# One core, gated linear attention into a gated FFN: all engines' orders, PSUM banks and holds laid out anew

## The chip, the cores and the metric

One core of a Trainium2 chip runs the program. It has five engines with instruction queues of their own: PE (TensorE, matmuls), DVE (VectorE), ACT (ScalarE), POOL (GpSimd) and SP (SyncE, here for DMAs only). The time is the device time of one execution in microseconds; the median of three executions is compared.

## What is computed

Two stages; the output of the first is the input of the second.

```python
B, H, S, D = 4, 8, 768, 48
f = 1.0 / (1.0 + np.exp(-f_logit))
for t in range(S):
    state = f[:, :, t, :, None] * state + np.einsum('bhd,bhe->bhde', k[:, :, t], v[:, :, t])
    y[:, :, t] = np.einsum('bhd,bhde->bhe', q[:, :, t], state)
...
x = attn_out.transpose(0, 2, 1, 3).reshape(3072, 384)
gate = np.maximum(x @ w_gate, 0.0)
val = x @ w_val
return gate * val @ w_out
```

d_model is 384, d_ff is 1536, all inputs are float32.

## The kernel before

**Tiling.** The 768 positions are cut into six chunks of 128. Chunk c of batch b is one piece of work, named by two digits (12 is chunk 1, batch 2). Chunks 0 and 1 are handled in *units* of two pieces: unit 0.0 is pieces 00 and 01, unit 0.2 is 02 and 03, then 1.0 and 1.2. Each unit needs one load of 384 KB of each of f, k, q and v (`load`, L407 for these, L412 for later chunks). The weights come in ten *slices* (`load_w`, L434), all issued by POOL: wg0+2 is columns 0 and 1 (of 12 blocks of 128) of w_gate, wv4+4 is blocks 4 to 7 of w_val, wo is w_out.

**Stages of a piece**, with the names that the orders use:

- `ef`, `ln` (ACT, L483 and L486): log of the forget gate, for two pieces at once; `cum` (PE, L504 or L513): its running sum
- `ek`, `eq` (ACT, L527 and L529): exponentials of the sum; `hk`, `hq` (POOL or DVE, L551 or L552): k and q scaled by them, called hats
- `tk`, `tq` (PE, L563) and `ck`, `cq` (DVE or ACT): transposes and their copies, chunks 0 and 1 only; later chunks use a DMA transpose `xh` (SP, L571)
- `s` (PE, L661 or L595): scores; `m` (DVE): masks; `v` (POOL, DVE or ACT, L581 to L583): v cast to bfloat16
- `kv` (PE): the state's update, `st`, `ss`, `sd`: the new state; `y`, `yi` (PE, L683, L719, L756): the output; `x`: its copy, turned, as input of the FFN
- `g` and `u` (PE, L803): the two projections of a hidden block, 00.6 being block 6 of all of chunk 0; `r` (ACT or DVE): the relu, `p` (DVE, L811): the product; `o` (PE, L824): the output projection in three parts; `d` and `S`: its copy and its store

In chunk 0 blocks 0 to 3 are done for two pieces at a time (256 columns, names g00.x and g02.x, *narrow*), all others for four (512 columns, *wide*).

**Order.** Every instruction group is an `Op` with a number. `ORDER` lists for each engine which numbers it runs, in which order. Engines run strictly in that order. From it `Plan.lay_out` (L153) takes the engine of each Op, and `BANKS` says which of the eight PSUM banks each newly opened result of PE takes; an Op that opens a bank waits for whoever still reads the bank's last tenant. `Plan.waits` (L187) works out the semaphore waits. `HELD` adds waits that the data do not need: an Op number and the Op that it is held for. An entry like ~4512 in PE's list is a *filler* (L884 to L890): four matmuls of 512 columns on zeros, whose result is thrown away; before a filler PE waits for the readers of the bank it writes. The list starts with ~60100, 60 fillers of 100 columns.

**Loads.** In the kernel before, SP and ACT send unit loads at the same time: SP f0.0, q0.0, f0.2, v0.2, k0.2, f1.0, f1.2, q1.2, then k1.0, q1.0, k1.2; ACT v0.0, k0.0, q0.2, ahead of its first arithmetic. k1.0 and k1.2 are held for slice wv4+4, f1.0 for wg2+2, v1.2 for wo0+4; five slices (wg0+2, wv0+2, wv2+2, wv4+4, wo0+4) are held for loads in turn.

Of the kernel before, what the change touches and what calls it, by code (L numbers as in the profile page):

```python
# [25 lines left out]
        45, ~60100, 85, 74, ~4512, 92, ~4512, 82, 90, 80, 101, ~3512, 95, 121, 110, ~7512, 100, 118, 104, 126, 128, 152, 156,  # L26
        137, 116, 230, 131, ~4512, 266, 148, 241, 150, 144, 146, ~2512, 136, 140, 277, 158, 154, 168, 170, 184, 164, 166,
# [13 lines left out]
    ],  # L41
    "ACT": [
# [8 lines left out]
    ],  # L51
    "DVE": [
# [901 lines left out]
```

## Time and profile before

| | us |
|---|---|
| median of 3 runs | 193.23 (192.92 to 193.8) |
| span of the profiled execution | 193.3 |
| granted TensorE clock | 1.000 of full speed |

The page gives the span from the first to the last instruction of the profiled execution and no other time for it; the span lies within 0.1 us of the runs' median. In 40 slices of 4.8 us each, busy tenths of PE and DVE, and GB/s moved:

```profile
PE   7889999879999999999999999999999999999994
...
DVE  5288867898968999758896779799788974585431
...
GB/s 148 285 319 265 170 196 212 149 219 245 209 238 188 233 198 254 172 178 231 242 180 233 212 235 225 173 215 91 108 196 120 2 41 0 46 0 81 41 43 123
```

PE is busy nearly all the time after the first nine slices. Matmuls are pipelined and fillers count as busy, so a busy PE is not yet a useful one. The chain of waits, read below, is the list of what released what, followed back from the last instruction. The view of a line's DMA issues gives the time from the issue to the landing.

### The profile page before, as it was taken

Reading aid. Unit: us, or ns where it says so; the run is one execution under the profiler, and the core shown is the slowest. Engines: PE = TensorE matmul, PEld = TensorE weight load, DVE = VectorE, ACT = ScalarE, POOL = GpSimd, SP = SyncE. Lnnn points to the kernel's source line nnn. Section 1 sums busy time; section 2 is a strip of 40 time slices with the busy share of each in tenths; the row PEclk is TensorE's granted clock in tenths of the full one; section 3 lists DMA queues with packets and bytes.
Section 4 is the critical chain, followed back from the end, with each engine's and each line's share of the span. In section 5 each row is a group of like instructions: output and inputs, shape, how many; then the busy total and the mean of one; then the engine's idle time right before and its main releaser. Section 6 shows DMA issues by size and latency. Waiting matters only on the chain.

```text
span 193.3 us, 4847 instructions
## 1 busy us (share of the span) xinstructions
PE 185.0 (96%) x1989; PEld 109.6 (57%) x2007; DVE 146.6 (76%) x271; ACT 86.7 (45%) x188; POOL 49.6 (26%) x78
## 2 busy tenths in 40 slices
PE   7889999879999999999999999999999999999994
PEld 7555675455565555655556565556655655555562
DVE  5288867898968999758896779799788974585431
ACT  2768963530388541588603797223352311113200
POOL 8368600420053300044623244161140000000000
PEclk9999999999999999999999999999999999999999
DMA  5999998699999999789999999896564010102113
GB/s 148 285 319 265 170 196 212 149 219 245 209 238 188 233 198 254 172 178 231 242 180 233 212 235 225 173 215 91 108 196 120 2 41 0 46 0 81 41 43 123
DMA packets 110279, 32.44 MB, mean 168 GB/s; under 512 B 103472, under 2 KB 110000, under 8 KB 110256
## 3 DMA queue, kind: packets, MB, share of 16 engines
q1 hardware_dynamic: 92032, 25.04, 60.2%
q0 software_dynamic: 3744, 3.54, 11.4%
q10 hardware_dynamic: 14480, 3.54, 8.1%
q8 instruction: 16, 0.26, 0.5%
q14 instruction: 7, 0.06, 0.1%
HBM read 25.95 MB, written 4.72 MB: 159 GB/s over the span
## 4 chain that ended last, share of the span: by engine, by line
PE 79%; DMA 11%; POOL 3%; ACT 2%; DVE 2%; issue 1%; SPq 0%; ACTq 0%
PE ps L803 41%; PE ps L824 25%; DMA wv<-in_moe_w_val_dram 5%; DMA q_in<-in_q_dram 4%; PE ps L595 2%; DMA f_in<-in_f_logit_dram 2%; PE ps L756 2%; POOL hats L551 2%; PE ps L513 2%; DVE hats L552 2%; PE ps L563 1%; PE ps L783 1%; PE ps L661 1%; PE ps L767 1%; POOL wg L434 1%
## 5 line engine op out<-in xcount | busy, mean ns | idle before, releaser
L811 DVE TENSOR_TENSOR gT<-relu,ps 128x512 bf16<-128x512 bf16 (+1 forms) x76 | 48.9, 654 | 15.8 <-PE ps L803 9.9
L803 PE MATMUL ps<-xT,wv 128*128 128x512 bf16 (+1 forms) x223 | 56.9, 368 | 0.4
L803 PE MATMUL ps<-xT,wg 128*128 128x512 bf16 (+1 forms) x218 | 55.4, 367 | 0.5
L824 PE MATMUL ps<-wo,gT 128*128 128x384 bf16 (+2 forms) x300 | 52.1, 320 | 0.0
L808 ACT ACTIVATE relu<-ps 128x512 bf16<-128x512 f32 (+1 forms) x42 | 23.9, 571 | 41.6 <-DVE gT L811 24.3
L824 PEld LDWEIGHTS ps<-wo,gT 128*128 128x128 bf16 x300 | 27.2, 98 | 18.7 <-DVE gT L811 0.6
L803 PEld LDWEIGHTS ps<-xT,wg 128*128 128x128 bf16 x228 | 23.6, 108 | 19.3 <-ACT xT L608 0.2
L803 PEld LDWEIGHTS ps<-xT,wv 128*128 128x128 bf16 x228 | 23.4, 108 | 18.7 <-ACT osb L830 0.5
L809 DVE TENSOR_SCALAR relu<-ps 128x512 bf16<-128x512 f32 (+1 forms) x34 | 22.3, 663 | 6.7 <-PE ps L803 5.9
L603 DVE TENSOR_TENSOR ptm<-ps,tri 128x512 bf16<-128x512 f32 x32 | 19.9, 683 | 2.6 <-PE ps L595 2.5
L459 POOL TENSOR_TENSOR st<-ssum,dec 128x384 bf16<-128x384 f32 x10 | 8.6, 856 | 33.4 <-DVE ssum L457 33.3
L551 POOL TENSOR_TENSOR hats<-q_in,expo 128x384 bf16<-128x384 f32 x13 | 13.7, 1060 | 12.8 <-ACT expo L529 8.1
L830 ACT ACTIVATE osb<-ps 128x384 f32<-128x384 f32 (+1 forms) x13 | 6.2, 480 | 21.2 <-PE ps L824 21.2
L529 ACT ACTIVATE expo<-ps 128x384 f32<-128x384 f32 x24 | 11.7, 496 | 7.9 <-PE ps L513 3.3
L551 POOL TENSOR_TENSOR hats<-k_in,expo 128x384 bf16<-128x384 f32 x11 | 11.4, 1038 | 13.2 <-ACT expo L527 10.2
L483 ACT ACTIVATE f_in<-f_in 128x768 f32<-128x768 f32 x12 | 10.0, 840 | 8.5 <-DMA f_in<-in_f_logit_dram 5.2
L552 DVE TENSOR_TENSOR hats<-k_in,expo 128x384 bf16<-128x384 f32 x13 | 10.9, 850 | 2.4 <-ACT expo L527 2.0
L527 ACT ACTIVATE expo<-ps 128x384 f32<-128x384 f32 x24 | 11.8, 499 | 1.5 <-PE ps L504 0.9
L552 DVE TENSOR_TENSOR hats<-q_in,expo 128x384 bf16<-128x384 f32 x11 | 7.0, 642 | 5.7 <-ACT expo L529 4.8
L888 PE MATMUL ps<-zeros 128*128 128x100 bf16 (+1 forms) x81 | 10.7, 309 | 0.3 <-issue 0.2
L668 DVE TENSOR_TENSOR ptm<-ps,tmask 128x512 bf16<-128x512 f32 x16 | 10.0, 683 | 0.6 <-PE ps L661 0.6
L486 ACT ACTIVATE bneg<-f_in 128x768 bf16<-128x768 f32 x12 | 10.1, 838 | 0.1
(79 smaller groups left out, 161.6 us busy)
## 6 DMA issues: line engine op xcount, KB each, us to landing
out_dram<-osb SPq DMA_DIRECT2D x23, 192.0 KB, 2.5
f_in<-in_f_logit_dram SPq DMA_DIRECT2D x10, 384.0 KB, 6.3
q_in<-in_q_dram SPq DMA_DIRECT2D x10, 384.0 KB, 5.9
k_in<-in_k_dram SPq DMA_DIRECT2D x10, 384.0 KB, 5.4
v_in<-in_v_dram SPq DMA_DIRECT2D x9, 384.0 KB, 5.8
v_in<-in_v_dram ACTq DMA_DIRECT2D x3, 384.0 KB, 5.1
k_in<-in_k_dram ACTq DMA_DIRECT2D x2, 384.0 KB, 6.7
q_in<-in_q_dram ACTq DMA_DIRECT2D x2, 384.0 KB, 7.7
```

The source lines that it names most:

```text
L486: add(f"ln{c}{b0}", by("ACT", lambda: sc.activation(bo, fl, AF.Ln, bias=1.0), act_(n)), keys + [f"bneg{bi}"], [f"bn{bi}_{x % 2}" for x in ...
L527: add(f"ek{c}{b}", by("ACT", lambda: sc.activation(ex[:, 1, :], bc.ap[:, 0:HD], AF.Exp, scale=1.0), act_(HD)), [bc], [f"expk{ei}"], key=P + 1)
L529: add(f"eq{c}{b}", by("ACT", lambda: sc.activation(ex[:, 0, :], bc.ap[:, 0:HD], AF.Exp, scale=-1.0), act_(HD)), [bc], [f"expq{ei}"], key=P ...
L551: return {**by("POOL", lambda: gp.tensor_tensor(o, i_, e_, ALU.mult), pool_(HD)), **by("DVE", lambda: ve.tensor_tensor(o, i_, e_, ALU.mult ...
L552: **by("DVE", lambda: ve.tensor_tensor(o, i_, e_, ALU.mult), dve_(HD))}
L603: add(f"m{c}{b}{j}", by("DVE", lambda b=b, j=j, mi=mi: ve.tensor_tensor(ptm[mi][:, j, :, :], s[b, j].ap[:, :].rearrange("p (n t) -> p n t" ...
L803: z = te.matmul(bank.ap[:, 0:n], wt[:, kt, w_cols(j)], xT[xi][:, kt, n0:n1], start=(kt == 0), stop=(kt == NK - 1))
L808: add(f"r{c}{b0}.{j}", {**by("ACT", lambda: sc.activation(rdst, gate.ap[:, 0:n], AF.Relu), act_(n)), **by("DVE", lambda: ve.tensor_scalar_ ...
L809: **by("DVE", lambda: ve.tensor_scalar_max(rdst, gate.ap[:, 0:n], 0.0), dve_(n))}, [gate], [f"relu{ri}"], key=P)
L811: add(f"p{c}{b0}.{j}", by("DVE", lambda: ve.tensor_tensor(gT[gi][:, j, n0:n1], rdst, val.ap[:, 0:n], ALU.mult), dve_(n)), [val, f"relu{ri} ...
L824: z = te.matmul(o.ap[:, 0:e1 - e0], gT[gi][:, j, b * C:(b + 1) * C], wo[:, j, e0:e1], start=(j == 0), stop=(j == NJ - 1))
L888: te.matmul((op.opens[0].ap if op.opens else banks[7])[:, 0:fill % 1000], zeros[:, 0:128], zeros[:, 0:fill % 1000], start=True, stop=True, ...
```

## The change

Only the three tables change; no Op is added or removed and none computes anything else. 11 of the 24 wide fillers go. The number of Ops per engine: DVE 271 to 266, POOL 74 to 82, ACT 180 to 179, SP 88 to 86, PE the same.

```diff
 ORDER = {
     "PE": [
-        45, ~60100, 85, 74, ~4512, 92, ~4512, 82, 90, 80, 101, ~3512, 95, 121, 110, ~7512, 100, 118, 104, 126, 128, 152, 156,
-        137, 116, 230, 131, ~4512, 266, 148, 241, 150, 144, 146, ~2512, 136, 140, 277, 158, 154, 168, 170, 184, 164, 166,
+        45, ~60100, 85, 74, ~3512, 110, 90, ~2512, 80, 121, 82, 92, ~3512, 95, 116, 126, 128, ~2512, 101, ~1512, 118,
+        ~1512, 100, 104, 230, 131, 266, 152, ~1512, 148, 137, 241, 144, 136, 140, 238, 158, 156, 172, 160, 154, 186,
...
     "POOL": [
-        41, 40, 25, 1, 36, 37, 38, 2, 4, 3, 13, 5, 7, 14, 8, 11, 56, 16, 39, 17, 20, 26, 94, 84, 79, 52, 120, 106, 125, 51,
-        57, 114, 62, 63, 69, 68, 142, 70, 71, 281, 280, 262, 298, 416, 382, 385, 408, 424, 441, 560, 558, 525, 566, 532, 565,
+        41, 25, 7, 39, 13, 16, 4, 26, 11, 38, 8, 1, 14, 5, 56, 17, 20, 78, 114, 36, 124, 2, 3, 37, 94, 84, 40, 115,
+        51, 57, 130, 63, 120, 52, 235, 62, 68, 106, 69, 70, 245, 71, 234, 244, 281, 280, 270, 276, 385, 262, 383, 390,
...
     "SP": [
-        46, 48, 50, 55, 53, 58, 64, 66, 59, 60, 65, 374, 61, 222, 517, 510, 373, 370, 212, 217, 803, 375, 384, 425, 417, 227,
+        46, 50, 47, 48, 53, 54, 49, 58, 55, 60, 59, 66, 368, 372, 371, 370, 212, 369, 375, 374, 373, 514, 510, 384,
...
 HELD = {
-    51: 53, 52: 50, 57: 53, 58: 56, 59: 63, 63: 58, 65: 63, 67: 70, 70: 60,
+    372: 378, 516: 343,
 }
```

The same in names, up to where the prediction walks (loads start with L; ~n is n wide fillers):

```text
SP before:   Lf0.0 Lq0.0 Lf0.2 Lv0.2 Lk0.2 Lf1.0 Lf1.2 Lq1.2 Lk1.0 Lq1.0 Lk1.2 Lq2.2 Lv1.0 S02
SP after:    Lf0.0 Lf0.2 Lk0.0 Lq0.0 Lk0.2 Lq0.2 Lv0.0 Lf1.0 Lv0.2 Lq1.0 Lk1.0 Lq1.2 Lf2.0 Lf2.2
             Lv2.0 Lq2.0 S00
ACT before:  Lv0.0 Lk0.0 Lq0.2 ef00 ln00 ek01 eq01 ek00 eq00 dc00 cq01 ef02 ck00 ln02 v03 ek03 eq03
ACT after:   ef00 ln00 ef02 ek01 ln02 ek00 eq01 eq00 ek02 eq03 ek03 cq00 Lf1.2 eq02 dc02 ck03 ef10
             dc00 ln10 ef12 ln12 x01 ek10 dc12 eq10 dc10 ek12 r00.2 r00.1 eq12 r00.0 x03 ek11 eq11
             eq13 r02.3 Lk1.2 r00.4 ek13 r00.6 r00.8 r00.11 ck11 cq13 ef20 ln20 Lv1.0 Lv1.2 ek20
             eq21 eq20 dc20 dc21 v10 ek21 d01 v13 d00 ef22 ln22 x12 x13 x10
DVE after:   (constants) hk01 mdec1 al1 hq00 hq01 ck00 cq01 ck01 hq03 m011 m001 m010 cq03 m000 cq02
             st00 ss10 ck02 x00 m031 m020 m030 m021 st01 x02 cq10
POOL before: (constants) wg2+2 (constants) v01 v00 hq00 wv0+2 v02 sd10 hq03 wg0+2 wv2+2 hk02 wg4+4
             wv4+4 wv8+4 wg8+4 sd11 wo0+4 wo4+8 hq13 hk13
POOL after:  (constants) wg2+2 (constants) hk00 hk02 mvpad0 hk03 stri mones mvpad1 v01 v00 mvpad4
             hq02 wg0+2 wv2+2 v03 wv4+4 v02 wv0+2 hq10 wg4+4 wg8+4 sd10 wv8+4 wo0+4 hq11 wo4+8 hk10
             hk11 hq13 hk13 hk12 v12
PE before:   cum01 cum00 ~4 tq01 ~4 tq00 tk01 tk00 kv00 ~3 s00 cum03 cum02 ~7 y00 tq02 yi01 tk03
             tq03 g00.2 g00.3 kv02 tk02 cum10 s02 ~4 cum12 g00.1 cum11 u00.1 g00.0 u00.0 ~2 y02 yi03
             ... g00.10 tk13 u00.10 tk11 tq12 u00.9 o00.0 s12
PE after:    cum01 cum00 ~3 cum02 tk01 ~2 tk00 cum03 tq00 tq01 ~3 s00 tk02 tk03 tq03 ~2 kv00 ~1
             tq02 ~1 y00 yi01 cum10 s02 cum12 g00.2 ~1 g00.1 kv02 cum11 g00.0 y02 yi03 tq10 u00.3
             g00.3 g02.3 g02.0 u00.2 u00.6 g02.2 cum13 u00.0 u00.1 u02.3 u02.1 u02.2 g02.1 u02.0
             u00.4 g00.5 g00.7 g00.4 tk10 tq11 g00.6 u00.7 u00.5 g00.9 g00.8 tq13 g00.11 g00.10
             tk11 tk12 tk13 tq12 u00.9 u00.8 u00.11 s12 u00.10 o01.0 o00.0 o02.0 cum20 cum21 ...
             kv12 kv10 y12 yi13 y10 yi11 cum22 o03.8 u10.3
```

The two holds of the new kernel: the load f2.2 waits for the sum cum20, and the load q3.2 for a product of chunk 1 (p10.10). ACT issues eleven loads, one of unit 1.2 early (f1.2) and ten from between its later work: k1.2, v1.0, v1.2, f4.0, f4.2, q3.0, k3.0, f5.0, v4.2, k5.0. The rest of the lists, and BANKS, are new throughout and follow the same stages.

94 rows, old and new, of tables (BANKS, ORDER) are left out of this document.

## The prediction

> **What bounds the kernel now.** I read the busy shares first, then the same shares in two stretches, then the chain of waits, and last the timelines of PE and GpSimd (POOL) in the first 45 us. The first two rows are the page's busy part; the next two are windows (length, then busy time and count of PE, PEld, DVE, ACT, POOL, the granted clock, DMA share, GB/s); the last is the filler line alone, from 7 us on.
>
> ```profile
> span 193.3 us, 4847 instructions
> PE 185.0 (96%) x1989; PEld 109.6 (57%) x2007; DVE 146.6 (76%) x271; ACT 86.7 (45%) x188; POOL 49.6 (26%) x78
> ...
> 7.00:45.00 38.00, 34.91 (x511) 21.65 (x517) 30.35 (x55) 23.11 (x52) 14.36 (x17) 1.00 1.08 221
> 45.00:191.00 146.00, 144.85 (x1419) 82.85 (x1429) 113.32 (x193) 60.48 (x133) 29.62 (x33) 1.00 0.74 153
> ...
> L888 PE MATMUL ps<-zeros 128*128 128x512 bf16 x21 | 5.5, 379 | 0.3 <-issue 0.2
> ```
>
> From 45 us to the end PE idles 146.00 - 144.85 = 1.15 us in all. So PE sets the time, and no order can win more than about a microsecond there. Between 7 and 45 us it is busy 34.91 of 38 us, but 5.5 us of that is matmuls on zeros that compute nothing: 38 - 34.91 + 5.5 = 8.6 us bring no result. That is what a new order can win from, with the start ahead of it. The matmuls that count are the same before and after.
>
> ```profile
> 0.81 4.33 DMA f_in<-in_f_logit_dram
> 5.16 0.85 ACT f_in L483
> 6.04 0.85 ACT bneg L486
> ...
> 7.03 0.50 PE ps L504 x2
> ...
> 9.27 1.35 POOL hats L551
> ...
> 12.82 0.64 PE ps L661 x32
> ...
> 19.34 8.96 DMA wv<-in_moe_w_val_dram
> ...
> 28.32 0.37 SPq L407
> ...
> 28.73 7.33 DMA q_in<-in_q_dram
> ...
> 36.09 1.03 DVE hats L552 x2
> ...
> 37.71 0.59 DVE gT L811
> 38.31 1.95 DVE hats L552
> ...
> 40.92 0.65 PE ps L803 x3
> 41.57 0.22 PE ps L563 x4
> ...
> 42.89 0.65 PE ps L803 x3
> 43.54 0.65 PE ps L824 x4
> 44.19 0.57 PE ps L661 x32
> ```
>
> This is the chain of waits (start, length, what). Its second half says why the load phase is long: SP holds k1.0 until the slice wv4+4 has landed (19.34 + 8.96), only then sends k1.0 and q1.0, q1.0 lands at 36.1, and hats, transposes and the last hidden matmuls follow. The hidden layer of chunk 0 ends at 42.89 + 0.65 = 43.54 us. I use that as the mark: the work behind it is PE-bound.
>
> **The change, step by step.** It moves instructions; the only ones gone are 11 of the 24 wide fillers. They stand where PE waits, so their 11 x 0.217 = 2.4 us are no gain of their own: what counts is when the operand comes. I walk the new orders with durations of the profiled execution; times are from its start.
>
> ```profile
> 1.34 5.16 PE L888 MATMUL ps<-zeros 128*128 128x100 bf16 x60
> 20.55 0.64 PE L661 MATMUL ps<-qkT 48*64 48x128 bf16 x32
> 23.27 0.49 PE L803 MATMUL ps<-xT,wv 128*128 128x256 bf16 x3
> 23.59 0.49 PE L803 MATMUL ps<-xT,wg 128*128 128x256 bf16 x3
> 24.77 0.73 PE L683 MATMUL ps<-ptm,vpad 64*32 64x128 bf16 x64
> ...
> 15.96 0.80 POOL L434 DMA_DIRECT2D wg<-in_moe_w_gate_dram  x1
> ...
> q1 hardware_dynamic: 1699, 0.64, 115.5%
> ...
> L551 POOL TENSOR_TENSOR hats<-k_in,expo 128x384 bf16<-128x384 f32 x11 | 11.4, 1038 | 13.2 <-ACT expo L527 10.2 <-DMA k_in<-in_k_dram 1.9 <-issue 1.0
> ```
>
> 1. *The first f.* The loads of unit 0 were spread over SP and ACT; now SP alone sends f0.0, f0.2, k0.0, q0.0, k0.2, q0.2, v0.0 and so on. The q1 row is SP's queue from 12 to 14 us, alone: 0.64 MB in 2 us, so a unit load (384 KB, 0.39 MB) takes 1.2 us of it. Without v0.0 beside it f0.0 lands up to 1.2 us sooner (3.9 to 5.1). But the 60 narrow fillers end at 1.34 + 5.16 = 6.50, so the first cumulative sum starts at 6.53 at best against 7.03: 0 to 0.5 us. I take 0.5.
>
> 2. *Unit 0.* ACT now does the second f (0.85 and 0.85) between the first exponentials, which uses up part of that; hk00 goes to POOL (1.35) and hq00 to DVE. hk00 ends near 10.0, the four transposes near 10.9, their copies near 11.8, and the scores (L661) start at about 11.9 against 12.82. v0.0 is seventh in the queue and lands near 12; POOL casts it at 12.8 to 13.8, behind hk02 and hk03, which it has to do anyway. The masks on DVE end at 15.3, so v's delay is covered by about 1.5 us, and y00 starts near 15.5. The second unit's scores start near 17.1 (20.55 before).
>
> 3. *POOL paces the weights.* The holds on loads and slices are gone: POOL issues a slice when it gets there. After hq02 (14.0 to 15.0) come wg0+2 at 15.0 (15.96 before), wv2+2 15.8, a cast, wv4+4 17.1, a cast, wv0+2 18.4, hq10, wg4+4 21.0, wg8+4 21.8, a state product, wv8+4 23.5, wo0+4 24.3, hq11, wo4+8 26.1. k1.0, q1.0 and k1.2, which went out from 28 us on, now run beside these slices. Landing times of slices and loads, from the issues' view (KB, median us to landing) and the two load lines:
>
> ```profile
> wg<-in_moe_w_gate_dram POOLq DMA_DIRECT2D x2, 192.0 KB, 6.0
> wv<-in_moe_w_val_dram POOLq DMA_DIRECT2D x2, 384.0 KB, 9.5
> ...
> DMA to landing us min/median/max: 4.9/7.5/11.2
> ...
> DMA to landing us min/median/max: 4.3/7.3/13.2
> ...
> DMA to landing us min/median/max: 3.8/5.6/8.5
> ```
>
> The third row is all ten weight slices (L434), the fourth the unit loads (L407), the fifth the later loads (L412).
>
> 4. *PE to the mark.* g00.2 runs near 18.8, behind ln12 on ACT. g00.1 needs wg0+2: 15.0 + 6.0 = 21.0, a wait of about 1.7 us that did not exist. Then g00.1 0.33, kv02 0.45, cum11 0.34, g00.0 0.33, y02 0.67, yi03 0.28, one transpose group 0.22 and five narrow projections at 0.33 (the start distance 23.59 - 23.27): 25.3. u00.6 needs wv4+4: by the chain's own slice 17.1 + 8.96 = 26.1; bounds 17.1 + 6.0 = 23.1 (no wait) and 17.1 + 11.2 = 28.3 (the longest slice). I take the chain's own, the slice of the same name and size. From u00.6 to the last hidden matmul u00.10 stand 16 wide projections (0.65), 8 narrow (0.33), 7 transpose groups (0.22), a sum (0.18) and scores (0.57): 15.3 us. g00.5 needs wg4+4 (21.0 + 9.5 = 30.5) and waits 0.3. So u00.10 ends at 26.1 + 15.3 + 0.3 = 41.7. The scores s12 (0.57) stood behind the mark before, so like for like it is 41.2 against 43.54: **2.3 us won**. q1.0 and k1.0 are no limit any more: they are tenth and eleventh on SP and land by about 20, even at a third of the rate beside slices, while hk10 on POOL is at 27.
>
> 5. *DVE and ACT.* POOL takes eight more operations (six hats, two casts net), DVE five fewer, ACT about as many. DVE's part between u00.6 and the mark is 12 wide relus and products at 0.6 (the chain's 0.59), 9 narrow ones at half of that, six copies, one hat and one state product: about 13 us of 15.3, so it can follow; if it could not, PE would stall on PSUM banks, which the 30.35 of 38 us busy before shows it did not.
>
> 6. *Behind the mark.* PE cannot win more than the 1.15 us. New are: SP sends f2.2 only after the first sum of unit 2.0 (near 44.0), and ACT has to do ef22 and ln22 ahead of the copies x12, x13, x10 that the next hidden layer needs; and ACT issues ten later loads in the stream of its relus. With the median 5.6 the copies are done near 52.9 (44.1 + 5.6 + 1.7 + 1.5) and PE wants them at 53.7. Bounds for this part: -1.15 (all idle gone) to +2.1 (landing 8.5). I charge 0.6, near the middle.
>
> The sum: 193.3 - 2.3 + 0.6 = **191.6**. The page gives the span only; the runs' median is 193.23, so span and time agree within 0.1 and I leave it at 191.6.
>
> **The rivals.**
>
> *Slower: k1.2 comes last.* ACT, not SP, now sends k1.2, behind eq13 and r02.3, and eq13 needs the sum cum13 that stands behind u00.6. So it goes out at 26.1 + 1.2 + 0.4 + 0.3 = 28.0, beside the heaviest slices. hk12 (1.04 on POOL) and the transposes tk12 follow, which PE reaches at 37.9: it must land within 8.8 us. The median is 7.3, the longest 13.2. At 13.2 PE stalls 4.4 us: 196.0. Above 10.5 the whole gain is gone; between, it is a loss of part of it. For it speaks how loads fare beside slices, here from 18 to 20 us (queue: packets, MB, share):
>
> ```profile
> q0 software_dynamic: 576, 0.29, 113.0%
> ...
> q1 hardware_dynamic: 290, 0.11, 19.3%
> ```
>
> The load got 0.11 MB in 2 us, at which 0.39 MB take 7 us before any fixed part. Against it: by 32 us most slices should be in.
>
> *No change: f2.2 late.* Step 6 at its upper end, +2.1 instead of +0.3 of the 0.6: 193.4. The point is a landing over 6.4 us after its issue.
>
> *Faster: slices land early.* If wv4+4 and wg4+4 need no wait (25.3 + 15.3 = 40.6) and the later idle stays as it was, 191.6 - 1.1 - 0.6 = 189.9. Against it: the slices of 384 KB took about 9 us and more, by their median and by the chain's one.
>
> *Slower by the clock.* The wait at 19 to 21 us is longer than any that PE had after 7 us:
>
> ```profile
> 40.30 0.62 PE L563 MATMUL ps<-ident,hats 128*128 128x128 bf16 x8 [0.97 <-DVE hats L552]
> ```
>
> If PE then ran at the rate of its first fillers (5.16/60 = 86 ns for 100 columns, against 0.65/3 = 217 ns for 512, that is 42 ns for 100), the 4.3 us up to u00.6 would take 8.6, less the 0.8 that it waits there anyway: 195.1. The Trainium skill, TensorE: Matmul & The Clock Gate, "Part 1: The HAM clock gate", has the rule: an idle window of about 3.4 us halves TensorE's clock until it has been busy as long again. By that rule a wait of 1.7 us is too short to do it, and the fillers that were taken out were not needed; no run here yet shows a wait of this length.
>
> *It doesn't do what it says.* f alone may win nothing, since the fillers end at 6.50; that is inside step 1 (0.5 us either way).
>
> **How the numbers follow.** Forecast 0.42, with its own range 190.6 to 192.6; faster rival 0.10; f2.2 late 0.10; clock 0.05; k1.2 late 0.33, since it has a margin of only 1.5 us over the median and the same wait can arise at any slice whose landing I took at its median. A measurement of this kernel can't tell less than about 0.5% (1.0 us) from no change. Faster than 192.3: nearly all of the forecast and the faster rival, 0.49. Within 0.5%: f2.2 late and the lower part of k1.2, 0.18. Slower: the rest of k1.2 and the clock, 0.33. The range leaves one in ten on each side: 189.8 to 195.2.
>
> **What would show it.** Right: no PE gap near 36 to 40 us; a PE wait on wg near 19 to 21 and on wv near 25 to 26; last hidden matmul of chunk 0 near 41.7; PE idle of about 1 to 2 us behind it. Wrong in step 2: scores of unit 0 not before 12.8. Wrong in step 3: wv4+4 landing over 28. The k1.2 rival: PE or its weight loads waiting on POOL's hats near 38 to 42. The f2.2 rival: PE waiting on ACT's xT near 53. The clock: matmuls of 512 columns 0.43 us apart.

## The result, and the profile after

The changed kernel takes **202.54 us** (median; 201.18 to 204.44) against 193.44 for the kernel before on the same chip: a ratio of **1.045** (1.041 to 1.050). Forecast were 191.6 and a range of 189.8 to 195.2. It is 9 us slower, and the time lies outside the range. Medians here are over all executions; ratios leave out those that lie more than 1.5% above the fastest of their kernel (here 204.44).

A base has to be put right first. In nearly every timed execution the reported time is about 1.8 us more than the span (after: 203.12 against 201.3). The profile of before that the prediction worked from has a span of 193.3; the unchanged kernel was profiled again among the experiments, and there a time of 193.47 goes with a span of 191.6. The first profile was thus an execution 1.7 us longer than usual. I compare with the second, called *before, again*. The profiled execution of after has a span of 201.3; its other executions have 199.4 to 202.6, so the shares below are those of one execution.

The page of the changed kernel (span; busy tenths of PE and its granted clock in 40 slices of 5 us):

```profile
span 201.3 us, 4800 instructions
...
PE   7868969909999999999999999799999999999994
...
PEclk9999999975999999999999999999999999999999
```

PE's row has one 0, at 40 to 45 us, and the clock falls in the same slice and the next. The same in windows (length, then busy time and count of PE, PEld, DVE, ACT, POOL, clock, DMA share, GB/s), first after, then before, again:

```profile
7.00:30.00 23.00, 17.82 (x373) 10.69 (x370) 15.26 (x31) 14.28 (x36) 17.31 (x27) 1.00 1.16 243
30.00:45.00 15.00, 10.18 (x69) 6.37 (x67) 8.20 (x18) 5.43 (x9) 3.24 (x4) 0.92 1.03 196
45.00:60.00 15.00, 14.28 (x144) 8.26 (x146) 9.59 (x18) 4.94 (x13) 1.41 (x3) 0.85 0.45 96
```

```profile
7.00:30.00 23.00, 22.02 (x398) 13.81 (x399) 17.06 (x32) 17.77 (x42) 10.54 (x13) 1.00 1.20 238
30.00:45.00 15.00, 15.00 (x131) 9.12 (x130) 13.83 (x27) 5.40 (x10) 3.74 (x4) 1.00 1.07 234
```

The loss arises between 30 and 60 us; from 60 to 110 PE is busy all 50 us at full clock. PE's timeline of after shows it (start, duration, count; in brackets the idle time before and what ended it):

```profile
13.04 0.64 PE L663 MATMUL ps<-qkT 48*64 48x128 bf16 x32 [0.20 <-DVE qkT L569]
...
22.02 0.50 PE L805 MATMUL ps<-xT,wg 128*128 128x256 bf16 x3
...
27.22 0.81 PE L805 MATMUL ps<-xT,wv 128*128 128x512 bf16 x3 [0.74 <-DVE gT L813]
...
29.71 1.80 PE L805 MATMUL ps<-xT,wv 128*128 128x256 bf16 x15 [1.19 <-DMA wv<-in_moe_w_val_dram]
...
45.72 1.44 PE L565 MATMUL ps<-ident,hats 128*128 128x128 bf16 x12 [5.54 <-POOL hats L553]
...
50.83 0.84 PE L805 MATMUL ps<-xT,wv 128*128 128x512 bf16 x3
...
130.62 0.62 PE L597 MATMUL ps<-qkT 48*128 48x128 bf16 x16 [1.15 <-DMA qkT<-hats]
```

PE waits 5.54 us for hats from POOL, and the chain of waits of after names what POOL waited for:

```profile
28.57 14.93 DMA k_in<-in_k_dram
...
43.63 1.96 POOL hats L553 x2
...
47.16 3.17 PE ps L805 x9
```

This is k1.2: sent by ACT at 28.57, as the prediction's rival had it (28.0), but 14.93 us under way. Behind the wait the clock is halved (last column but two, 0.50):

```profile
46.00:48.00 2.00, 2.00 (x14) 1.40 (x13) 1.66 (x4) 0.00 (x0) 0.51 (x1) 0.50 0.09 24
```

A matmul of 512 columns takes 3.17/9 = 0.35 us on average there, against 0.65/3 = 0.22 in the rows of before. From the transposes to the last hidden matmul pass 51.67 - 45.72 = 5.95 us. At the rates of before this work is 12 transposes (0.22 for each 4), 12 wide matmuls (0.65 for each 3) and the scores (0.57), together 3.83 us. So the clock cost 2.1.

The mark (last hidden matmul of chunk 0) is 51.67, like for like without the scores 51.10. In before, again it is 40.96 + 0.81 = 41.77:

```profile
40.96 0.81 PE L803 MATMUL ps<-xT,wv 128*128 128x512 bf16 x3
```

| of the 9.7 us between the spans 201.3 and 191.6 | us |
|---|---|
| wait for k1.2 | 5.5 |
| half clock behind it | 2.1 |
| rest of the load phase, up to the mark (9.3 in all) | 1.7 |
| behind the mark | 0.4 |

Why 15 us for 384 KB? The queues of after from 34 to 36 us and from 38 to 40 (packets, MB, share of the engines; q0 carries POOL's slices, q10 ACT's loads):

```profile
q0 software_dynamic: 261, 0.31, 88.2%
q10 hardware_dynamic: 258, 0.10, 26.5%
...
q0 software_dynamic: 136, 0.37, 94.3%
q10 hardware_dynamic: 135, 0.05, 15.1%
```

Both queues move the same number of packets in each window (194 and 197 from 36 to 38 us), but those of the slices carry 1.2 to 2.7 KB and those of k1.2 about 0.38 KB, so k1.2 moves 0.025 to 0.05 MB a microsecond. That is not the whole of the 14.93 us: ACT's queue q10 moves nothing from 28 to 32 us, and what holds the first packets for over 3 us is not shown. The Trainium skill, DMA: Bandwidth & Descriptors, "Queues, rings and completion order", says that each DMA engine takes turns between the queues at the grain of a packet; the equal counts agree, as far as the packets of the trace are those of the rule. The runs add that a load of short packets then starves beside long ones.

### The profile page after: what moved, and what is told of

Its sections match the earlier page's. It is cut to its first block, busy times and chain, and to the rows that moved or that the text cites. A ratio compares the mean times of both kernels' runs of the same rounds, so it can differ in the third digit from the quotient of the medians.

```text
span 201.3 us, 4800 instructions
## 1 busy us (share of the span) xinstructions
PE 185.3 (92%) x1996; PEld 109.5 (54%) x1996; DVE 139.8 (69%) x266; ACT 84.1 (42%) x185; POOL 56.0 (28%) x86
## 4 chain that ended last, share of the span: by engine, by line
PE 72%; DMA 16%; POOL 3%; ACT 3%; DVE 2%; issue 1%; SPq 1%; ACTq 0%; POOLq 0%; DVEq 0%
PE ps L805 38%; PE ps L826 23%; DMA k_in<-in_k_dram 7%; DMA q_in<-in_q_dram 4%; DMA qkT<-hats 3%; DMA wg<-in_moe_w_gate_dram 3%; POOL hats L553 2%; PE ps L597 2%; PE ps L758 1%; PE ps L515 1%; SPq L409 1%; PE ps L685 1%; PE ps L565 1%; DVE gT L813 1%; PE ps L769 1%
## 5 line engine op out<-in xcount | busy, mean ns | idle before, releaser
L813 DVE TENSOR_TENSOR gT<-relu,ps 128x512 bf16<-128x512 bf16 (+1 forms) x76 | 47.9, 654 | 12.4 <-PE ps L805 8.6
L805 PE MATMUL ps<-xT,wg 128*128 128x512 bf16 (+1 forms) x228 | 53.7, 368 | 0.1
L810 ACT ACTIVATE relu<-ps 128x512 bf16<-128x512 f32 (+1 forms) x43 | 24.2, 581 | 39.7 <-PE ps L805 22.8
L826 PEld LDWEIGHTS ps<-wo,gT 128*128 128x128 bf16 x300 | 27.7, 98 | 18.2
L805 PEld LDWEIGHTS ps<-xT,wv 128*128 128x128 bf16 x228 | 23.9, 109 | 21.9 <-issue 1.7
L811 DVE TENSOR_SCALAR relu<-ps 128x512 bf16<-128x512 f32 (+1 forms) x33 | 21.2, 655 | 11.4 <-PE ps L805 11.2
L553 POOL TENSOR_TENSOR hats<-k_in,expo 128x384 bf16<-128x384 f32 x17 | 16.8, 1000 | 30.7 <-DMA k_in<-in_k_dram 16.8
L565 PE MATMUL ps<-ident,hats 128*128 128x128 bf16 x64 | 6.4, 237 | 7.0 <-POOL hats L553 5.5
L833 DVE COPY osb<-ps 128x384 f32<-128x384 f32 (+1 forms) x12 | 6.1, 531 | 7.5 <-PE ps L826 7.5
L583 POOL CAST vpad<-v_in 128x384 bf16<-128x384 f32 x11 | 5.8, 536 | 19.4 <-DMA v_in<-in_v_dram 16.2
L459 DVE TENSOR_TENSOR ssum<-ps,st 128x384 f32<-128x384 f32 x16 | 8.7, 551 | 3.2 <-PE ps L785 3.1
```

The lines of the kernel that those rows point to most:

```text
L553: return {**by("POOL", lambda: gp.tensor_tensor(o, i_, e_, ALU.mult), pool_(HD)), **by("DVE", lambda: ve.tensor_tensor(o, i_, e_, ALU.mult ...
L805: z = te.matmul(bank.ap[:, 0:n], wt[:, kt, w_cols(j)], xT[xi][:, kt, n0:n1], start=(kt == 0), stop=(kt == NK - 1))
L810: add(f"r{c}{b0}.{j}", {**by("ACT", lambda: sc.activation(rdst, gate.ap[:, 0:n], AF.Relu), act_(n)), **by("DVE", lambda: ve.tensor_scalar_ ...
L811: **by("DVE", lambda: ve.tensor_scalar_max(rdst, gate.ap[:, 0:n], 0.0), dve_(n))}, [gate], [f"relu{ri}"], key=P)
L813: add(f"p{c}{b0}.{j}", by("DVE", lambda: ve.tensor_tensor(gT[gi][:, j, n0:n1], rdst, val.ap[:, 0:n], ALU.mult), dve_(n)), [val, f"relu{ri} ...
L826: z = te.matmul(o.ap[:, 0:e1 - e0], gT[gi][:, j, b * C:(b + 1) * C], wo[:, j, e0:e1], start=(j == 0), stop=(j == NJ - 1))
```

## The experiments

Numbers in the diffs are those of the order lists. "Before" beside a time is the kernel before in the same batch. The experiments follow in the order of the questions: is it k1.2, what made k1.2 slow, were the prediction's other readings right, and what keeps the mended kernels above the kernel before.

### k1.2 sent by SP

```diff
 "ACT"
-  279, 173, 65, 177, 278
+  279, 173, 177, 278
 "SP"
-  55, 60, 59, 66, 368
+  55, 60, 59, 65, 66, 368
```

> Changed kernel, but SP sends the load k1.2 right behind k1.0 (about 16 to 18 us) in place of ACT at 28.6. Theory A (all that was lost is k1.2's lateness: 5.5 us of waiting and a halved TensorE clock behind it): the wait of 5.54 us before tk12 is gone, the granted clock stays 1.00, the last hidden matmul of chunk 0 ends near 44 instead of 51.7, span about 193.6. Theory B (the DMA queues as a whole are late: 0.39 MB sent sooner only push f2.0, q1.2 or a weight slice back, and another wait takes the place): span 196 or more, with a new PE wait on a slice or on q1.2 between 30 and 45 us.

Measured: median 198.26 (193.9 to 200.3; before 193.06), in four executions that lie far apart. The wait for k1.2 is gone and the mark comes at 43.81; the profiled execution (198.18) shows another gap:

```profile
85.78 0.24 PE L758 MATMUL ps<-ptm,vpad 128*32 128x128 bf16 x4 [2.94 <-issue]
```

It stands in the middle of an output group and no signal of any engine ends it. Its cause is followed below.

### k1.2 early on ACT

```diff
 "ACT"
-  122, 83, 64, 112
+  122, 83, 64, 65, 112
...
-  279, 173, 65, 177, 278
+  279, 173, 177, 278
```

> Changed kernel, but ACT sends k1.2 right behind its first load f1.2 (about 12 us). Theory A (the point is when k1.2 is sent, not by whom): the wait before tk12 is gone and the span is about 193.6, within 1 us of the kernel with k1.2 on SP. Theory B (ACT's queue is what is slow, or ACT pays for a second issue before its own work): f1.2 lands later, ln12 and g00.2 move from 21.2 to 23 or later, span 195 or more.

Measured: 196.35 (194.38 to 197.17), ratio 1.016 (1.010 to 1.022). From PE's timeline and the chain of this kernel:

```profile
22.37 0.50 PE L805 MATMUL ps<-xT,wg 128*128 128x256 bf16 x3 [2.11 <-DMA wg<-in_moe_w_gate_dram]
...
29.52 1.80 PE L805 MATMUL ps<-xT,wv 128*128 128x256 bf16 x15 [0.21 <-DMA wv<-in_moe_w_val_dram]
```

```profile
43.94 1.95 PE ps L826 x12
```

The mark (the start of the output projection) comes at 43.94 instead of 51.67: 7.7 us, as much as wait and half clock together (5.5 + 2.1). Up to the narrow projections the two kernels are level (29.52 here, 29.71 in after), although this one has a wait of 2.11 us with half clock behind it; the difference arises after that. k1.2's late landing is the cause of most of the loss. What remains is 1.6 us in the load phase and gaps behind the mark.

### Fillers in the wait

24 wide fillers (5.2 us) on PE ahead of tk12, so that PE isn't idle while it waits.

```diff
 "PE"
-  200, 246, 272, 282
+  200, 246, ~24512, 272, 282
```

> Changed kernel with 24 wide fillers on PE ahead of the transposes tk12, so that PE is busy while it waits for k1.2. Nothing else moves. Theory A (behind the stall TensorE's clock is halved, which costs about 2.1 us: tk12 to u00.10 took 5.95 us against 3.83 at full rate): clock 1.00 in all slices, span near 199.2. Theory B (those matmuls are slow because their operands come late, not by the clock): span unchanged at 201.3 or more. Theory C (fillers run into the time when tk12 could start): over 202.

Measured: 204.45, ratio 1.058 (1.055 to 1.061).

```profile
45.67 0.84 PE L565 MATMUL ps<-ident,hats 128*128 128x128 bf16 x12 [0.60 <-POOL hats L553]
...
63.66 0.23 PE L721 MATMUL ps<-qkT,st 128*32 128x128 bf16 x2 [2.84 <-issue]
```

k1.2 is as late (tk12 at 45.67), yet the mark comes at 49.80, 1.9 us sooner: twelve transposes take 0.84 instead of 1.44. The granted clock stays at 1.00 from 44 to 52 us. That isolates the price of the half clock: 1.9 of the 2.1 worked out above. The time did not follow, because a gap without a signal of 2.84 us appears at 63.66, with its own stretch of half clock.

### The slices of w_out behind hk12

```diff
 "POOL"
-  106, 69, 70, 245, 71, 234, 244, 281, 280, 270, 276
+  106, 69, 245, 234, 244, 281, 280, 270, 70, 71, 276
```

> The two slices of w_out, which POOL issues at 26.5 and 28.2 us in the changed kernel, go out behind hk12. Theory: k1.2 took 14.9 us because its packets of 384 bytes took turns, one for one, with the much larger packets of the slices; without the last two slices it lands near 38 (9 to 10 us after its issue at 28.6), the wait before tk12 shrinks from 5.5 us to under 1, no stretch of half clock follows, the hidden layer of chunk 0 ends near 44 to 45 instead of 51.7, and the time falls to 195.5 to 197.5. Rival: k1.2 is slow because it is sent by ACT's queue, or because of the slices issued before it; then it still lands past 42 and the time stays over 200. w_out itself is needed only near 45: if it is now late, PE waits on it before the first output projection.

Measured: 199.32 (198.38 to 201.82; before 193.6), ratio 1.028 (1.025 to 1.032). Chain and PE's timeline of this kernel:

```profile
28.30 8.81 DMA k_in<-in_k_dram
```

```profile
40.04 0.83 PE L565 MATMUL ps<-ident,hats 128*128 128x128 bf16 x12 [1.02 <-POOL hats L553]
...
49.25 2.77 PE L826 MATMUL ps<-wo,gT 128*128 128x384 bf16 x16 [1.39 <-DMA wo<-in_moe_w_out_dram]
```

Sent by the same engine at nearly the same time, k1.2 lands in 8.81 us instead of 14.93, and PE waits 1.0. So the late slices starved it, and ACT's queue alone doesn't explain the 14.93. The mark comes at 44.2, as expected. The time is over the expected 195.5 to 197.5, though: behind the mark PE waits 0.42, then 1.39 for w_out, which now comes late, and 1.03 near 125.7 (1.15 in after). The rest of the excess is not accounted for.

### The kernel before without the holds on k1.0 and k1.2

```diff
 HELD
-  51: 53, 52: 50, 57: 53, 58: 56, 59: 63, 63: 58, 65: 63, 67: 70, 70: 60,
+  51: 53, 52: 50, 57: 53, 58: 56, 63: 58, 67: 70, 70: 60,
```

> The kernel before with two holds taken off: k1.0 and k1.2 no longer wait for slice wv4+4. Theory A (the prediction's: the holds are what makes the load phase of the kernel before long): q1.0 lands some 10 us sooner, the waits of PE near 36 to 41 us go, span about 191.8. Theory B (the holds protect the slices: a slice and a load side by side move 0.20 MB per us instead of 0.32): slices wg4+4 and wv4+4 land 2 to 4 us later, PE waits for them near 26 to 30 us, span 194 to 197.

Measured: 193.32, ratio 1.001 (0.999 to 1.004). No difference: in the usual execution of before PE idles 0 of 15 us between 30 and 45 (the window above). The prediction's reading of its chain of waits, that these holds make the load phase long, does not hold.

### The kernel before, again

> The kernel before once more, unchanged, for a second profiled execution: the first one had a span of 193.3 us, while the spans of the timed executions are near 191.3. If that first execution was a slow one, then here span near 191.3, last hidden matmul of chunk 0 near 42 instead of 43.5, and q1.0 in before 36. If not, span 193 again.

Measured: 193.12 (192.86 to 193.67), span 191.6 at 193.47. Its windows and mark are the ones shown above.

### v0.0 back with the first f

The kernel with k1.2 early on ACT, and v0.0 at the head of ACT's list again.

```diff
 "ACT"
-  72, 73, 108
+  49, 72, 73, 108
 "SP"
-  53, 54, 49, 58
+  53, 54, 58
```

> Kernel with k1.2 early on ACT, and v0.0 sent by ACT at the start, beside f0.0, as in the kernel before: undoes that f, q and k of the first unit go alone. Theory A (their going alone brings the first sums 0.7 us forward, but PE then waits for slices anyway): the first sums start near 6.9 instead of 6.2, last hidden matmul of chunk 0 within 0.5 us of 43.9, time within 0.7 us of 196.4. Theory B (v0.0 late is what makes POOL's casts and so its slices late): wg0+2 goes out sooner than 16.0, the mark comes 1 us sooner, time near 195.4.

Measured: 195.41 (193.59 to 197.16, 10 executions; before 193.19), ratio 1.008 (1.005 to 1.012). The first sums start at 6.98 instead of 6.18, but the mark comes 1.0 sooner (42.91 against 43.94).

```profile
28.49 1.80 PE L805 MATMUL ps<-xT,wv 128*128 128x256 bf16 x15 [0.24 <-DMA wv<-in_moe_w_val_dram]
```

The way there is POOL's: a cast of v that waited 1.31 us for its load in the kernel with k1.2 early doesn't wait here, so the slice wv0+2 goes out at 19.58 instead of 20.58, and PE, which waits for it in both kernels, goes on at 28.49 instead of 29.52. Sending f, q and k alone wins 0.8 us at the first sum and loses more behind it.

### All early slices sooner

The kernel with k1.2 early on ACT, wg0+2, wv2+2 and wv4+4 ahead of POOL's masks and casts.

```diff
 "POOL"
-  20, 78, 114, 36, 124, 2, 3, 37, 94, 84, 40, 115, 51, 57, 130, 63, 120
+  20, 78, 51, 114, 57, 36, 124, 2, 3, 37, 94, 84, 40, 63, 115, 130, 120
```

> Kernel with k1.2 early on ACT, and POOL issues wg0+2 and wv2+2 right behind its first two hats (near 9.5 and 11.5) and wv4+4 behind the casts, instead of at 16.0, 16.8 and 19.4. Theory A (the slices' pace on POOL is what still costs at the mark: PE waits for them at 21, 24, 26 and 29 us): those waits shrink, last hidden matmul of chunk 0 about 1 us sooner (near 42.9), time near 195.4. Theory B (slices sooner take their bandwidth from the unit loads, which PE needs first): q0.2, v0.0 or k1.0 land later, scores of the first units later than 11.8 and 18.4, time 196.4 or more.

Measured: 195.75 (194.82 to 197.63), ratio 1.016 (1.009 to 1.023), the same as without the change. The wait on wg0+2 is gone, but PE now waits 1.27 us for the unit's new state, and the mark gains only 0.4 (43.53):

```profile
19.65 0.35 PE L721 MATMUL ps<-qkT,st 128*32 128x128 bf16 x12 [1.27 <-DVE st L455]
```

Two things eat the gain. ACT waits for the load f1.0 until 17.9 instead of 15.1, and the state hangs on what ACT does next: beside the sooner slices the load came later. And the granted clock is 0.50 from 21 to 23 us, behind a wait of only 1.27.

### Shifting PE's instructions

The kernel with k1.2 on SP, and 100 first fillers of 60 columns for 60 of 100: same time, 40 matmuls more ahead of everything.

```diff
-  45, ~60100, 85, 74
+  45, ~100060, 85, 74
```

> Kernel with k1.2 on SP, and the 60 narrow fillers of 100 columns at the start made into 100 fillers of 60 columns: the same time at the start, but every later PE instruction stands 80 instructions (40 weight loads, 40 matmuls) further down PE's stream. Theory A (the gap of 2.9 us in the middle of y20 at 82.8 us, where PE waits for nothing, is PE's instruction fetch behind full DMA queues): that gap goes or moves to another place, and the time differs from 198.3 by 1 us or more, up or down. Theory B (it is an operand or a bank that the profile does not name): the gap stays within y20 near 82.8 and the time stays near 198.3.

Measured: 198.21 (197.25 to 200.53), ratio 1.024 (1.020 to 1.028). The gap at 85.78 is gone and another has come (besides, PE waits 2.38 us at 28.77 for a slice, and both waits have half clock behind them):

```profile
59.18 0.24 PE L685 MATMUL ps<-ptm,vpad 64*32 64x128 bf16 x6 [2.47 <-issue]
```

Its place can be counted. In the kernel with 24 fillers the gap stood ten matmuls into yi11 (two of twelve left). Here 40 matmuls stand ahead instead of 24, and it stands 16 earlier: six before the end of y10, which precedes yi11. This speaks for a place in PE's instruction stream and against an operand; the last experiment tests it.

### Transposes ahead of stores

The kernel with v0.0 at the head; on SP xh32 and xh33 ahead of the stores S12 and S11.

```diff
 "SP"
-  362, 559, 357, 567
+  559, 567, 362, 357
```

> The kernel with k1.2 early and v0.0 at the head of ACT's queue, and besides on SP the two DMA transposes xh32 and xh33 ahead of the two stores S12 and S11 (as the kernel before has xh33 ahead of its store). Theory: the 1.05 us that PE waits at 123.4 for the transposed hats comes from the store queued ahead of xh33; it goes to under 0.2, and the time falls by about 1.0 from 195.4 to 194.4 (193 to 196, since the gap at 83 stays). Rival: the transposes are late because the queues are full there; then the wait stays near 1 us and so does the time.

Measured: 195.01 (194.09 to 196.98; before 193.6), ratio 1.008 (1.005 to 1.011).

```profile
22.43 0.64 PE L805 MATMUL ps<-xT,wg 128*128 128x256 bf16 x3 [1.82 <-DMA wg<-in_moe_w_gate_dram]
...
83.73 0.24 PE L758 MATMUL ps<-ptm,vpad 128*32 128x128 bf16 x4 [1.08 <-issue]
123.76 0.62 PE L597 MATMUL ps<-qkT 48*128 48x128 bf16 x16 [1.06 <-DMA qkT<-hats]
```

The wait near 123 is unmoved. The expectation was aimed at the wrong chunk: the scores there are s42 and read xh42, not xh32 and xh33.

### Three loads back to SP's queue

The last kernel, with f4.2, q3.0 and k3.0 sent by SP.

```diff
 "ACT"
-  518, 519, 656, 512, 551, 361, 552, 356, 660, 511, 351
+  518, 519, 551, 361, 552, 356, 660, 351
 "SP"
-  217, 227, 516, 515, 352
+  217, 227, 656, 512, 516, 515, 511, 352
```

> As the last, and the three loads f4.2, q3.0 and k3.0 go back from ACT's queue to SP's, at the place where they were issued in time (72 to 78 us). Theory: PE's gaps of 0.6 to 2.9 us that end in no signal are waits for its next block of instructions, whose DMA takes turns with the load queues; with two full load queues (SP and ACT) beside it instead of one it comes too late. Then the gap near 83 goes, as in the kernel before, whose loads go out on SP alone at that place, and the time falls to 192.5 to 193.5 and scatters less. Rival: the gap depends only on where the blocks fall in the instruction stream; then it stays at about 1 us, within 1 us of its place, and the time stays at 194.4.

Measured: 194.62 (194.15 to 196.6), ratio 1.007 (1.004 to 1.010). The gap near 83 is gone in the profiled execution (span 192.4), but the median fell by 0.4 only, with overlapping intervals: not settled by this run.

### The kernel before with two load queues

f4.0, f4.2 and k3.0 go from SP to ACT in the kernel before.

```diff
 "ACT"
-  361, 433, 438, 551, 356, 552
+  361, 433, 438, 652, 656, 551, 356, 511, 552
 "SP"
-  516, 362, 512, 652, 656, 511, 654
+  516, 362, 512, 654
```

> The kernel before, with three of its loads (f4.0, f4.2, k3.0), which SP sends between 78 and 82 us, sent by ACT at about the same times. Theory of two queues: PE's instruction blocks come late where two load queues are full, so PE gets a gap of 0.5 to 3 us that ends in no signal near 80 to 86 us, the median rises by 0.5 to 2 us (193.7 to 195.5), and the times scatter over more than 1.5 us. Rival, density: in this kernel the four dense outputs stand two by two with wide matmuls between them, so PE has time in hand; no gap, time within 0.5 us of the kernel before.

Measured: 198.37 (195.91 to 202.14; before 193.15), ratio 1.020 (1.017 to 1.024). Three DMA instructions moved, and the kernel before is as slow and as scattered as the first mended kernel. But the gap is not of the kind expected. ACT, PE and a window of this kernel:

```profile
80.28 3.17 ACTq L412 DMA_DIRECT2D k_in<-in_k_dram  x1
...
83.50 0.84 ACT L486 ACTIVATE bneg<-f_in 128x768 bf16<-128x768 f32 x1 [2.10 <-issue]
```

```profile
84.39 0.34 PE L513 MATMUL ps<-bneg,tri 128*128 128x384 bf16 x1 [2.55 <-ACT bneg L486]
```

```profile
86.00:88.00 2.00, 2.00 (x6) 0.76 (x5) 1.73 (x3) 1.52 (x8) 2.00 (x2) 0.50 1.41 217
```

Issuing k3.0 holds ACT for 3.17 us, the arithmetic behind it is late, PE waits 2.55 us and then runs at half clock. A load on an engine that computes costs what is queued behind it there. Whether two queues also delay PE's instructions stays open here, since that place shows no gap without a signal.

### Wide matmuls between the dense outputs

The kernel with the transposes ahead; o13.4, o10.8 and o13.8 between y22 and y21.

```diff
 "PE"
-  553, 364, 350, 520, 528, 437, 432, 404, 399, 561, 365, 442
+  553, 520, 528, 437, 432, 364, 350, 365, 404, 399, 561, 442
```

> As the kernel in which xh32 and xh33 go ahead of the stores (195.0; two load queues near 80 us), with the three output projections o13.4, o10.8 and o13.8 put between the outputs y22 and y21 on PE, 12 wide matmuls, 2.0 us: the four dense outputs then stand two by two, as before. Theory of density: 112 short matmuls in 1.5 us use up instructions faster than they come; with 2 us of wide matmuls in the middle the gap near 83 (1.08 us) goes to under 0.2, the time falls to about 194.0 and scatters less. Theory of two queues alone: the block is late wherever it falls, so a gap of about 1 us stays near 81 to 86.

Measured: 196.05 (195.54 to 196.85), ratio 1.015 (1.013 to 1.018).

```profile
84.19 0.30 PE L758 MATMUL ps<-ptm,vpad 128*32 128x128 bf16 x8 [0.43 <-issue]
```

The gap stands four matmuls earlier in the third output (eight left instead of four), as it must when the four of o13.8 now stand ahead. It is 0.43 long instead of 1.08, but at the old place it was 0.60, 1.42 and 2.94 in other kernels with the same order on PE, so the shorter length can't be put down to density. The time did not fall: a wait of 0.40 for x20 and short ones for masks come in. This is no cure.

### hq42 and hq43 first

The kernel with three loads back on SP; on POOL hq42 and hq43 ahead of hk41 and hq41.

```diff
 "POOL"
-  666, 583, 674, 675, 702, 710, 723
+  666, 583, 702, 710, 674, 675, 723
```

> As the kernel with f4.2, q3.0, k3.0 on SP's queue (194.6), and on POOL hq42 and hq43 ahead of hk41 and hq41. Theory: SP can send the transposes xh42 and xh43 only when hq42 and hq43 are done, at 115; now they are done 2 us sooner, xh42 lands before PE gets to s42, the wait of 0.9 us near 121.7 goes to under 0.2 and the time falls by about 0.8 to 193.8. Rival: the transposes wait for the DMA queues or s42 for its bank (the row names DVE's product), then the wait stays at 0.9.

Measured: 194.00 (193.37 to 195.04; before 193.15), ratio 1.005 (1.003 to 1.007). PE has no wait over 0.15 us between 30 us and the end, and s42 starts at once, where it had waited 0.91. So the microsecond near 123 came from POOL's order of hats, not from SP's order of stores.

### One slice sooner

The last, with wg0+2 ahead of the casts v01 and v00 and of hq02.

```diff
 "POOL"
-  2, 3, 37, 94, 84, 40, 115, 51, 57
+  2, 3, 37, 51, 94, 84, 40, 115, 57
```

> As the last, and POOL sends the slice wg0+2 ahead of the casts v01 and v00 and of hq02 (near 14 us instead of 16.2). Theory: it lands about 2 us sooner, PE's wait of 1.6 us on it at 22.5 goes, nothing else moves, and the time falls by 1 to 1.6 to 192.2 to 192.8. Rival: what the slice gains the unit's loads or the casts lose (as when all slices went sooner): PE waits for another operand between 15 and 30 us, and the time changes by under 0.5.

Measured: **193.38** (192.78 to 194.8, 10 executions; before 193.15), ratio 1.002 (0.999 to 1.004): level with the kernel before. The wait on wg0+2 is gone. Two gaps without a signal are what remains:

```profile
24.20 0.60 PE L685 MATMUL ps<-ptm,vpad 64*32 64x128 bf16 x48 [1.49 <-issue]
...
81.93 0.24 PE L758 MATMUL ps<-ptm,vpad 128*32 128x128 bf16 x4 [0.34 <-issue]
```

### Shifting the last kernel's instructions both ways

```diff
-  45, ~60100, 85, 74
+  45, ~100060, 85, 74
```

> As the kernel with the slice wg0+2 sent sooner (193.4), with 100 first fillers of 60 columns in place of 60 of 100: 40 matmuls more in PE's instruction stream, the same time. Theory of the instruction blocks: the gap of 1.49 us at 24.2 moves about 40 matmuls forward, to a place near 22 among the narrow projections, or goes; if no other block then falls among short matmuls the time is 192.0 (191.5 to 192.8). Rival: the gap belongs to y02 itself (an operand, a bank); then it stays where it is with the same length.

```diff
-  45, ~60100, 85, 74
+  45, ~40150, 85, 74
```

> The same with 40 first fillers of 150 columns: 20 matmuls less. Theory of the instruction blocks: the gap moves some 20 matmuls back, later into y02 or behind it, and stays about as long: 193 to 193.5. Rival: as above.

Measured: 200.93 (200.64 to 201.67; before 193.03) with 40 matmuls more, ratio 1.041 (1.038 to 1.044); 195.62 (193.71 to 196.0) with 20 less, ratio 1.010 (1.006 to 1.014). PE's timelines, with more and with less:

```profile
24.77 0.50 PE L805 MATMUL ps<-xT,wg 128*128 128x256 bf16 x3 [2.50 <-issue]
59.62 0.24 PE L685 MATMUL ps<-ptm,vpad 64*32 64x128 bf16 x6 [2.64 <-issue]
```

```profile
25.08 0.40 PE L685 MATMUL ps<-ptm,vpad 64*32 64x128 bf16 x28 [1.67 <-issue]
84.89 0.35 PE L758 MATMUL ps<-ptm,vpad 128*32 128x128 bf16 x12 [0.81 <-issue]
```

Unshifted, the first gap stood 16 matmuls into y02 (48 of 64 left). With 20 matmuls less ahead it stands 36 in (28 left): 20 later. With 40 more it stands ahead of g00.1, which with kv02, a sum and g00.0 makes 3 + 16 + 1 + 3 = 23 matmuls up to y02: 16 + 23 = 39 earlier. The second gap moves likewise, from four left in the third output to twelve left in the fourth (4 + 12 + 4 = 20 later), and with more fillers it is the very one of the earlier shift, six before the end of y10. The operand theory falls. That the gaps are waits for PE's instructions is inferred: a queue for instructions (q8) moves 16 packets of 16 KB in the whole execution of after (0.26 MB), and one of them runs just ahead of such a gap, or where it begins (with 40 more: packets between 22 and 23 and between 56 and 57 us, gaps from 22.3 and 57.0). Whose instructions a packet carries is not shown. Transposes ahead, from 80 to 82 us (the gap is from 82.6 to 83.7):

```profile
q10 hardware_dynamic: 1167, 0.22, 70.5%
q1 hardware_dynamic: 1097, 0.21, 65.8%
q8 instruction: 1, 0.02, 4.0%
```

With 40 more the time rises by 7.5 us although the gaps sum to only 5.1 against 1.8: each is followed by half clock (window behind the first; behind the second it is 0.50 from 60 to 63):

```profile
26.00:28.00 2.00, 2.00 (x80) 1.29 (x78) 0.46 (x2) 0.46 (x2) 1.56 (x3) 0.50 1.29 179
```

## Why the prediction was wrong

The step that failed is step 4 of the prediction, "PE to the mark", in what it left out: it walked the slices up to u00.6 and u00.10 and put the wait for k1.2, whose transposes stand ahead of u00.10, at nothing. Measured, this wait is 5.54 us, and the half clock behind it 2.1. It stood aside as a rival at 0.33, on a median landing of 7.3 us against the 8.8 that were left.

- **The rival** had the right place and chain: sent at 28.0 (28.57), hk12, tk12 wanted at 37.9 (40.2), PE waiting on POOL's hats. It was mis-sized. The longest landing of the old kernel, 13.2, was taken as its bound, and a quoted row (0.11 MB in 2 us) gave 7 us. That row was no rate beside slices: 261 of its 290 packets ran in the first of the two microseconds, then SP's queue was all but empty. With w_out's slices beside it the rate was 0.10 MB in 2 us at 34 us and 0.05 at 38, and the landing 14.93. "By 32 us most slices should be in" was the wrong sentence: POOL was still sending the last at 28.17, and the queue moved 0.37 MB from 38 to 40. At 5.54 the wait is 1.1 over the 4.4 that were the worst case.
- **The clock** was a rival of its own, at 0.05, tied to the wait for wg0+2. In after it came behind the wait for k1.2 instead (2.1 us). The rival's own wait came in the mended kernels: half clock followed it at 1.82 and 2.11 us, not at 1.39, 1.60 and 1.64.
- **The base.** "Span and time agree within 0.1" was chance: time is span plus 1.8, and the profiled execution was 1.7 us longer than usual. Its mark, 43.54, is 41.77 in the usual one, so the 2.3 us to be won were 0.6 by the same walk (41.2).
- **The holds.** "Its second half says why the load phase is long" was read from waits that the usual execution doesn't have; without the two holds the time is the same.
- **Step 1** had the first sum at 6.53 at best, because the narrow fillers end at 6.50 in the first profile. They end at 5.68 in before, again and at 5.94 in after, and the sum starts at 6.19 against 7.02: 0.8 us won, not 0.5. **Step 2** had the scores L663 at 11.9. They start at 13.04 in this execution, behind a late hat, but at 11.74 and 11.77 in two kernels with the same orders up to there (slices of w_out behind hk12; k1.2 sent by SP). The second unit's scores are late in all three: 19.63, 19.54 and 18.25 for 17.1. And undoing v0.0's move wins 1.0 us at the mark.
- **Step 3.** POOL issues 1.7 to 2.3 us later than walked (wg0+2 16.71 for 15.0, wv4+4 19.11 for 17.1, wo4+8 28.17 for 26.1). g00.1 and u00.6 follow 1.0 and 1.1 late (22.02, 27.22), and then comes a wait of 1.19 on wv0+2 that the walk didn't have.
- **Step 5** held: PE waits 0.74 for DVE at u00.6, and from there to the mark no wait of PE of 0.15 us or more ends in DVE or ACT.
- **Step 6**, 0.6 behind the mark, is 0.4 by measurement, but not for its reason: no wait stands near 53; s42 waits 1.15 at 130.6 for its transposed hats.

## What to carry to other kernels

Before a load is put behind paced weight slices, walk it to its consumer like any operand, with the bytes per packet of what runs beside it: here a load with packets of 0.38 KB got a third to a seventh of the bytes of the slices beside it. Size a stall with the half clock that can follow it, and profile the base twice before its waits are read as causes. A DMA issued by an engine that computes holds what stands behind it there: one issue on ACT took 3.17 us. SP, which computes nothing here, had no such work to hold up.

## What the runs showed of the hardware

**Half clock after less than 2 us.** Windows of the kernel with the transposes ahead (a wait of 1.82 us at 22.4), and one of the kernel with one slice sooner (1.49 at 24.2):

```profile
22.00:24.00 2.00, 1.57 (x20) 0.95 (x21) 0.32 (x2) 0.98 (x3) 1.98 (x4) 0.67 1.30 198
24.00:26.00 2.00, 2.00 (x77) 1.29 (x78) 0.46 (x2) 0.38 (x1) 2.00 (x3) 0.50 1.28 182
```

```profile
24.00:26.00 2.00, 1.80 (x71) 1.50 (x72) 1.02 (x2) 0.86 (x3) 2.00 (x3) 1.00 1.28 188
```

Waits of 1.67, 1.82, 2.11 and 2.38 to 2.84 us were followed by a stretch of half clock; those of 1.49, 1.60 and 1.64 were not, and neither was the one of 2.94 at 85.78. Two shorter waits were: 1.27 us at 19.65 with the slices sooner (0.50 from 21 to 23 us), and 1.14 at 15.39 with the slices of w_out behind hk12 (0.50 from 16 to 18). Both had another wait of under 1 us shortly before. So in these runs the length of one wait does not decide it. The prediction held a wait of 1.7 us too short for it, after the Trainium skill, TensorE: Matmul & The Clock Gate, "Part 1: The HAM clock gate", which puts the idle window at about 3.4 us and says that it runs free of the kernel. The runs differ on the length, since half clock followed waits well under 3.4 us. That the wait of 2.94 escaped and the one of 1.67 did not fits a window whose phase the kernel doesn't set, but no run here set the phase.

**Gaps at fixed places of the instruction stream**, 0.2 to 2.9 us, at or just ahead of stretches of short matmuls. Where the queues were read beside one (80 to 82 us above), two load queues kept the DMA engines busy. The gaps turn up in some kernels and not in others with the same order on PE (2.94 at 85.78 with k1.2 on SP, none there in after), and in the kernel before at none of those places. A change of order is also a change of what stands at those places.
